# Half order, output buffers and the last block's stores of a fused Fourier mixing and maxout kernel

## The chip, the cores and the metric

The kernel runs on one core of a Trainium2 chip. The metric is the device time of one execution in microseconds, as the median of several runs; lower is better. A core has five instruction streams: TensorE (PE; its weight loads are shown apart as PEld), VectorE (DVE), ScalarE (ACT), GpSimd (POOL) and SyncE (SP). DMA transfers are issued from the streams of SP, POOL and ACT.

## What is computed

The input x has 8 batches of 3072 positions with 256 features. The kernel takes the real part of the Fourier transform over both axes, and passes each of the 24,576 resulting rows through a feed-forward layer whose hidden units are the maximum of three projections.

```python
def _attn_ref(x):                       # x: (8, 3072, 256)
    X = np.fft.fft(x, axis=1)
    X = np.fft.fft(X, axis=2)
    return X.real.astype(np.float32)

def _moe_ref(x, w1, w2, w3, w_out):     # w1, w2, w3: (256, 768), w_out: (768, 256)
    h = np.maximum(np.maximum(x @ w1, x @ w2), x @ w3)
    return (h @ w_out).astype(np.float32)

def reference(x, w1, w2, w3, w_out):
    return _moe_ref(_attn_ref(x).reshape(-1, 256), w1, w2, w3, w_out)
```

## The kernel before

**Mirror symmetry.** For real input, row s of the transform over positions and its mirror row 3072 - s share an even part and differ in the sign of an odd part. So only 1536 of 3072 positions are transformed (plus the middle one, `l2_mid`), into two tables per batch: `tE` (even part) and `tO` (odd part), each 128 x 1536 in bf16. Wherever rows are produced, a "direct" half (even plus odd, names with p) and a "mirror" half (even with the odd sign turned, names with m) are computed from the same columns.

**The maximum rewritten.** Folded weights `gE`, `gO` (made at the start) hold the feature transform times w2 - w1 and w3 - w1. Then max(x w1, x w2, x w3) = x w1 + max(0, x (w2 - w1), x (w3 - w1)). The second summand is the hidden activation `hp` or `hm`; the first is linear, and w1 times w_out is folded into `gw` (columns 0 to 255 for the even part, 256 to 511 for the odd part of direct rows, 512 to 767 for that of mirror rows).

**Loops.** Each of 8 batches is worked in 3 blocks of 512 columns (`TOKB`), each block in 6 units, one for each 128 of the 768 hidden units (`jc`). A unit is:

- `unit_plus` (L384): 4 matmuls of 512 columns into the banks `pse2` and `pse3` (L390, L391).
- `unit_out` (L401): ScalarE writes relu(pse2) to `stmp` (L404), VectorE writes max(pse3, stmp) to `hp` (L405).
- `unit_minus` (L394), one unit later by `finish` (L608): 2 matmuls (L398) that turn the same two banks into the mirror rows' values, and `unit_out` again, into `hm`. pse2 and pse3 have two banks each, so the `unit_plus` of the unit after the next writes the banks of this one.

The unit's last mirror part runs inside the first unit of the next block (`prev` is carried over), except at the end of a batch, where `finish` is called ahead of the block's output work (L632).

**The second layer** of a block is a generator, `l2_block` (L418), put in `l2_queue` when the block's units are done; each following unit advances it by 10 steps (`l2_some(10)`, L623), one matmul to a step as a rule. So the output of a block is interleaved with the units of the next. A block has 4 tiles of 128 positions (`sub`). For two tiles at a time, the even linear part is multiplied into the bank `pl` (L432) and copied by ScalarE to `even` (L436). For each tile, one matmul of 512 columns puts the two odd linear parts into the bank `po` (L440: direct in columns 0 to 255, mirror in 256 to 511). `l2_hidden` (L412) adds 6 matmuls of 256 columns to each half (L414). VectorE adds `even` to both halves and writes the tile `ot` (L453), which has 4 buffers. Direct rows leave by a plain transfer from SP, one row in 24 (L468). Mirror rows come out in falling order, and leave by an indexed transfer from POOL, with row numbers from `rows_m` (L458), and a memset of one element behind it (L462).

In the last block of the last batch the tiles come in the order 2, 3, 0, 1, and the last tile's addition is split in halves (L446, L450).

**Around it.** All engines run in the order of the program text (`manual_schedule`). Between units, a table of due pieces (`plan`) interleaves the transform of the next batch: `Mix.s` (L323, matmuls on x), `Mix.fold` (L333, VectorE), `Mix.k` (L361 to L373). SP's stream carries the loads of x two to three batches ahead (`load_chunk`, L100) between the direct stores, and POOL's stream carries the casts of the loaded x to bf16 (`turn_chunk`, L118) between the indexed stores; an instruction that waits holds up what stands behind it.

The lines that matter below: L390, L398, L405 (units), L414, L440, L453, L458, L468 (output), L533 (`out_pool`), L634 (where a block's output is queued), L661 (the program's exit).

Of the kernel before, what the change touches and what calls it, by code (L numbers as in the profile page):

```python
# [9 lines left out]
FP32 = mybir.dt.float32  # L10
BF16 = mybir.dt.bfloat16
INT32 = mybir.dt.int32
AX = mybir.ActivationFunctionType
ALU = mybir.AluOpType
# [19 lines left out]
def kernel(  # L34
# [9 lines left out]
    nc = tc.nc  # L44

    B, S, D = x.shape
# [3 lines left out]
    TOKB = 512  # L50
# [35 lines left out]
    gw = consts.tile([128, 768], BF16, tag="gw")  # L86
# [73 lines left out]
    for jh in range(2):  # L160
        for wsrc, wdst in ((moe_w1, w1_bf), (moe_w2, w2_bf), (moe_w3, w3_bf)):
            wld = nc.gpsimd.dma_start(
                out=wdst.rearrange("p (fc j) -> p fc j", fc=2)[:, :, jh * 384:(jh + 1) * 384],
                in_=wsrc.rearrange("(fc p) j -> p fc j", fc=2)[:, :, jh * 384:(jh + 1) * 384])
        if jh == 0:
            first_half = wld
    nc.gpsimd.dma_start(out=wout_bf.rearrange("p (jc c) -> p jc c", jc=NJC),
                        in_=moe_w_out.rearrange("(jc p) c -> p jc c", jc=NJC))
# [14 lines left out]
    for (name, value) in (("half_pi", 0.5 * math.pi), ("rnd", ROUND), ("n24", -24.0),  # L183
                          ("n256", -256.0), ("n3072", -3072.0)):
        c = gen.tile([128, 1], FP32, name=name, tag=name)
# [24 lines left out]
        out=m24blk.rearrange("p (g r) -> p g r", g=4),  # L210
        in0=t24.unsqueeze(1).to_broadcast([96, 4, 24]),
        in1=ind24.unsqueeze(2).to_broadcast([96, 4, 24]), op=ALU.mult)
# [5 lines left out]
    for (r0, r1) in ((0, 7), (7, 13)):  # L218
# [3 lines left out]
            out=v[:, cs].rearrange("p (r j) -> p r j", j=128),  # L222
            in0=j128.unsqueeze(1).to_broadcast([128, n, 128]), scalar=pidx,
            in1=pi13[:, r0:r1].unsqueeze(2).to_broadcast([128, n, 128]),
# [14 lines left out]
    for fc in range(2):  # L239
# [3 lines left out]
            out=vm[:, fc * 256:(fc + 1) * 256].rearrange("p (k c) -> p k c", c=128),  # L243
            in0=dvec.unsqueeze(1).to_broadcast([128, 2, 128]), scalar=pf[:, fc:fc + 1],
            in1=half.rearrange("p (k c) -> p k c", c=128), op0=ALU.mult, op1=ALU.add)
# [138 lines left out]
    def unit_plus(te, to, jc, n):  # L384

        js = slice(jc * 128, (jc + 1) * 128)
        pse2 = ps_l1.tile([128, TOKB], FP32, name="pse2", tag="pse2")
        pse3 = ps_l1.tile([128, TOKB], FP32, name="pse3", tag="pse3")
        for (pse, i) in ((pse2, 0), (pse3, 1)):
            nc.tensor.matmul(pse[:, 0:n], gE[i][:, js], te, start=True, stop=False)  # L390
            nc.tensor.matmul(pse[:, 0:n], gO[i][:, js], to, start=False, stop=True)  # L391
        return pse2, pse3

    def unit_minus(pses, to, jc):  # L394

        js = slice(jc * 128, (jc + 1) * 128)
        for i, pse in enumerate(pses):
            nc.tensor.matmul(pse, gD[i][:, js], to, start=False, stop=True,  # L398
                             skip_group_check=True)

    def unit_out(pses, dst, n):  # L401
        stmp = h_pool.tile([128, TOKB], BF16, name="stmp", tag="stmp")
        src3 = pses[1][:, 0:n]
        nc.scalar.activation(out=stmp[:, 0:n], in_=pses[0][:, 0:n], func=AX.Relu)  # L404
        nc.vector.tensor_tensor(out=dst, in0=src3, in1=stmp[:, 0:n], op=ALU.max)  # L405

    def stored(st, mine, others):
        for group in others:
            tc.declare_no_dep(st.ins, group=group, reason="each store has rows of its own")
        tc.add_to_no_dep_group(mine, st.ins)  # L410

    def l2_hidden(po, hcols):  # L412
        for jc in range(NJC):
            nc.tensor.matmul(po, hcols(jc), wout_bf[:, jc * 256:(jc + 1) * 256],  # L414
                             start=False, stop=(jc == NJC - 1), skip_group_check=True)
            yield

    def l2_block(b, blk, hp, hm, te, to):  # L418

        base = b * S  # L420
        last = b == B - 1 and blk == 2
        order = (2, 3, 0, 1) if last else range(4)
        for k, sub in enumerate(order):
            slot = blk * 4 + sub
            r = slot + 1
            cp = slice(slot * 128, slot * 128 + 128)
            sp = slice(sub * 128, sub * 128 + 128)
            if k % 2 == 0:
                pl = ps_f.tile([128, 512], FP32, name="pl", tag="ps")
                for i in range(2):  # L430
                    ci = (slot + i) * 128
                    nc.tensor.matmul(pl[:, i * 256:(i + 1) * 256], te[:, ci:ci + 128],  # L432
                                     gw[:, 0:256], start=True, stop=True)
                    yield
                even = out_pool.tile([128, 512], FP32, name="even", tag="even")
                nc.scalar.copy(out=even, in_=pl)  # L436
            lin = even[:, (k % 2) * 256:(k % 2 + 1) * 256]
            po = ps_o.tile([128, 512], FP32, name="po", tag="po")
            ot = out_pool.tile([128, 512], FP32, name="ot", tag="ot")
            nc.tensor.matmul(po, to[:, cp], gw[:, 256:768], start=True, stop=True)  # L440
            yield
            yield
            split = last and k == 3
            yield from l2_hidden(po[:, 256:512], lambda jc: hm[:, jc, sp])
            if split:
                nc.vector.tensor_tensor(out=ot[:, 256:512], in0=po[:, 256:512], in1=lin,  # L446
                                        op=ALU.add)
            yield from l2_hidden(po[:, 0:256], lambda jc: hp[:, jc, sp])
            if split:
                nc.vector.tensor_tensor(out=ot[:, 0:256], in0=po[:, 0:256], in1=lin,  # L450
                                        op=ALU.add)
            else:
                nc.vector.tensor_tensor(  # L453
                    out=ot.rearrange("p (h c) -> p h c", h=2),
                    in0=po.rearrange("p (h c) -> p h c", h=2),
                    in1=lin.unsqueeze(1).to_broadcast([128, 2, 256]), op=ALU.add)
            lo = 1 if r == 12 else 0
            stored(nc.gpsimd.indirect_dma_start(  # L458
                out, bass.IndirectOffsetOnAxis(
                    ap=rows_m[0:128 - lo, b * 12 + slot: b * 12 + slot + 1], axis=0),  # L460
                ot[lo:128, 256:512], None), "scattered", ("scattered", "direct"))
            nc.gpsimd.memset(mark, 0.0)  # L462
            if r <= 11:
                stores = [(0, 128, base + r)]
            else:
                stores = [(0, 64, base), (64, 128, base + 12)]
            for (p0, p1, row) in stores:
                stored(nc.sync.dma_start(out=out[row: row + 24 * (p1 - p0 - 1) + 1: 24, :],  # L468
                                         in_=ot[p0:p1, 0:256]), "direct", ("scattered",))

    def l2_mid():

# [29 lines left out]
    l2_queue = []  # L502

    def l2_some(n):
        while n > 0 and l2_queue:
            try:
                next(l2_queue[0])
                n -= 1
            except StopIteration:
                l2_queue.pop(0)  # L510
# [19 lines left out]
    ps_l1 = ctx.enter_context(tc.tile_pool(name="ps_l1", bufs=2, space=bass.MemoryType.PSUM))  # L530
    ps_o = ctx.enter_context(tc.tile_pool(name="ps_o", bufs=2, space=bass.MemoryType.PSUM))
    h_pool = ctx.enter_context(tc.tile_pool(name="hbuf", bufs=2))
    out_pool = ctx.enter_context(tc.tile_pool(name="outbuf", bufs=4))  # L533
    second = [prep_first(1, nc.vector.tensor_copy,
                         lambda: ps_o.tile([128, 512], FP32, name="psg", tag="po")),
              prep_second()]
# [66 lines left out]
    for b in range(B):  # L603
        mm = mixes[b]
        tE, tO = mm.tE, mm.tO
        prev = None

        def finish(prev):  # L608
            pses, to, jc, hm = prev
            unit_minus(pses, to, jc)  # L610
            unit_out(pses, hm[:, jc, :], TOKB)

        for blk in range(3):
            cs = slice(blk * TOKB, (blk + 1) * TOKB)
            hp = h_pool.tile([128, NJC, TOKB], BF16, name="hp", tag="hp")
            hm = h_pool.tile([128, NJC, TOKB], BF16, name="hm", tag="hm")
            for jc in range(NJC):
                pses = unit_plus(tE[:, cs], tO[:, cs], jc, TOKB)
                unit_out(pses, hp[:, jc, :], TOKB)
                if prev is not None:  # L620
                    finish(prev)
                prev = (pses, tO[:, cs], jc, hm)
                l2_some(10)  # L623
                if b == B - 1 and blk == 0:
                    if jc == 0:
                        middle = l2_mid()
                    for _ in range(5):
                        next(middle, None)
                for fn in plan.get((b, blk * NJC + jc), ()):
                    fn()  # L630
            l2_some(1000)
            if blk == 2:  # L632
                finish(prev)
            l2_queue.append(l2_block(b, blk, hp, hm, tE, tO))  # L634

    l2_some(1000)

# [28 lines left out]
```

## Time and profile before

| what | value |
|---|---|
| median of 3 runs | 457.61 us (456.12 to 457.81) |
| the profiled execution | 458.86 us |
| its span, first to last instruction | 457.1 us |
| mean granted TensorE clock in it | 0.987 |
| output addition, L453, 128x512 | 95 times, 682 ns each |
| hidden maximum, L405, 128x512 | 288 times, about 690 ns each |
| indexed store, L458, on POOL | 96 times, 1101 ns each |
| plain store, L468, on SP | 88 of 128 KB, 16 of 64 KB |

The time holds some 1.8 us outside the span. Busy time is given by engine; an engine that is busy nearly all the time bounds the kernel. A group's idle time is what its engine stood still just before it, with the instruction that ended the wait behind an arrow. Where the page shows a matmul's duration, several overlap: what a matmul takes from TensorE is the distance between the starts of two. The granted clock is the share of full speed at which TensorE was let run; 1.00 is full speed.

### The profile page before, as it was taken

To read this page: it belongs to the slowest core of one execution; us is meant where nothing else is said; L and a number is where in the kernel's file an instruction comes from. 1 tells how busy PE (TensorE), PEld (TensorE's weight loads), DVE (VectorE), ACT (ScalarE), POOL (GpSimd) and SP (SyncE) were. 2 spreads that over 40 slices of the span, in tenths; PEclk is the share of its full clock that TensorE was granted. 3 is DMA by queue.
4 is the path that set the end of the run, shared out by engine and by line. 5 is a ranking of instruction groups with operands and counts; after the bars stand their busy time and mean duration, and the time that the engine had idled before them with its cause. 6 is when DMAs were issued, how large, how long until landed. Compare 5 with 4: busy or idle time off the path is not lost.

```text
span 457.1 us, 9213 instructions
## 1 busy us (share of the span) xinstructions
PE 417.3 (91%) x3240; PEld 276.0 (60%) x3240; DVE 309.2 (68%) x643; ACT 276.8 (61%) x518; POOL 236.4 (52%) x258
## 2 busy tenths in 40 slices
PE   0499999999999999999999999999899999999990
PEld 0275666766676666666666667666476666655660
DVE  7667568675966596667856687567756596676760
ACT  3577576657666676567565676667466676555530
POOL 7616632884279525971388326952279421223252
PEclk9999999999999999999999999999899999999996
DMA  9999996498219861697419851797411211112132
GB/s 114 131 156 134 138 182 157 105 176 150 96 66 166 144 156 57 116 168 133 127 60 167 162 146 48 117 157 138 121 37 70 65 74 50 70 59 70 70 105 58
DMA packets 127422, 51.59 MB, mean 113 GB/s; under 512 B 109704, under 2 KB 124304, under 8 KB 127376
## 3 DMA queue, kind: packets, MB, share of 16 engines
q1 hardware_dynamic: 104496, 35.41, 41.7%
q0 software_dynamic: 21296, 15.21, 17.0%
q10 hardware_dynamic: 1584, 0.39, 0.6%
q8 instruction: 25, 0.41, 0.4%
q14 instruction: 21, 0.17, 0.1%
HBM read 28.31 MB, written 25.17 MB: 117 GB/s over the span
## 4 chain that ended last, share of the span: by engine, by line
PE 54%; issue 17%; POOL 10%; DMA 8%; DVE 5%; ACT 3%; SPq 1%; POOLq 0%; ACTq 0%; DVEq 0%
PE po L414 16%; PE pse L390 8%; PE pse L391 8%; PE pse L398 8%; POOL out_dram L458 7%; DMA xs<-in_x_dram 6%; PE ps L323 4%; DMA out_dram<-ot 3%; POOL x L118 2%; PE po L440 2%; DVE hm L405 2%; ACT stmp L404 1%; PE ps L361 1%; PE ps L370 1%; PE psg L270 1%
## 5 line engine op out<-in xcount | busy, mean ns | idle before, releaser
L404 ACT ACTIVATE stmp<-pse 128x512 bf16<-128x512 f32 x288 | 167.6, 604 | 62.1 <-PE pse L391 56.8
L458 POOL DMA_INDIRECT out_dram<-ot,rows_m x96 | 105.7, 1101 | 185.2 <-DVE ot L453 177.6
L405 DVE TENSOR_TENSOR hp<-pse,stmp 128x512 bf16<-128x512 f32 x144 | 99.4, 690 | 111.1 <-ACT stmp L404 67.6
L118 POOL CAST x<-xs 96x2048 bf16<-96x2048 f32 x28 | 105.9, 3782 | 19.6 <-DMA xs<-in_x_dram 17.5
L390 PE MATMUL pse<-tE,gE 128*128 128x512 bf16 x288 | 109.2, 379 | 0.6 <-DVE hm L405 0.2
L391 PE MATMUL pse<-tO,gO 128*128 128x512 bf16 x288 | 109.1, 379 | 0.0
L405 DVE TENSOR_TENSOR hm<-pse,stmp 128x512 bf16<-128x512 f32 x144 | 98.6, 685 | 8.4 <-ACT stmp L404 8.2
L414 PE MATMUL po<-wout_bf,hm 128*128 128x256 bf16 x576 | 89.3, 273 | 8.8 <-DVE hm L405 8.8
L398 PE MATMUL pse<-tO,gD 128*128 128x512 bf16 x288 | 86.1, 381 | 0.0
L414 PEld LDWEIGHTS <-hm 128*128 128x128 bf16 x576 | 56.4, 98 | 40.1 <-DVE hm L405 13.5
L414 PE MATMUL po<-wout_bf,hp 128*128 128x256 bf16 x576 | 79.2, 274 | 0.5 <-DVE ot L446 0.5
L325 ACT CAST ub<-ps 128x480 bf16<-128x480 f32 (+1 forms) x102 | 51.5, 559 | 40.5 <-PE ps L323 40.5
L453 DVE TENSOR_TENSOR ot<-po,even 128x512 f32<-128x512 f32 x95 | 64.8, 682 | 5.9 <-PE po L414 3.4
L414 PEld LDWEIGHTS <-hp 128*128 128x128 bf16 x576 | 56.7, 98 | 17.5 <-issue 1.2
L398 PEld LDWEIGHTS <-gD 128*128 128x128 bf16 x288 | 27.9, 98 | 32.2
L391 PEld LDWEIGHTS <-gO 128*128 128x128 bf16 x288 | 28.1, 98 | 20.3 <-issue 2.1
L390 PEld LDWEIGHTS <-gE 128*128 128x128 bf16 x288 | 28.6, 99 | 19.2 <-issue 0.4
L440 PE MATMUL po<-gw,tO 128*128 128x512 bf16 x96 | 36.6, 382 | 0.0
L323 PE MATMUL ps<-m24blk,x 96*128 96x96 bf16 x512 | 33.0, 216 | 2.5 <-DVE dif L254 1.5
L323 PEld LDWEIGHTS <-x 96*128 96x128 bf16 x512 | 30.1, 111 | 4.8 <-DVE dif L254 2.4
L436 ACT COPY even<-pl 128x512 f32<-128x512 f32 x48 | 28.4, 592 | 3.3 <-PE pl L432 3.0
L373 ACT CAST tO<-ps 128x512 bf16<-128x512 f32 x24 | 14.1, 586 | 24.5 <-PE ps L370 24.5
(113 smaller groups left out, 324.7 us busy)
## 6 DMA issues: line engine op xcount, KB each, us to landing
xs<-in_x_dram SPq DMA_DIRECT2D x112, 192.0 KB
out_dram<-ot SPq DMA_DIRECT2D x88, 128.0 KB
out_dram<-ot,rows_m POOLq DMA_INDIRECT x96, 3.9
w_bf<-in_moe_w_dram POOLq DMA_DIRECT2D x6, 192.0 KB, 4.4
out_dram<-ot SPq DMA_DIRECT2D x16, 64.0 KB
xs<-in_x_dram SPq DMA_DIRECT2D x8, 96.0 KB
x<-in_x_dram POOLq DMA_DIRECT2D x8, 96.0 KB, 11.8
xs<-in_x_dram ACTq DMA_DIRECT2D x4, 96.0 KB
```

The lines of the kernel that those rows point to most:

```text
L118: cast = nc.gpsimd.tensor_copy(turned[b][:, :, ch * 32:(ch + 1) * 32], raw.pop((b, ch)).rearrange("p (bb dl) -> p dl bb", dl=64))
L323: nc.tensor.matmul(ps1[:, i * 96:(i + 1) * 96], x0[:, d0 + i, :], m24blk, start=True, stop=True)
L325: evict(out=self.ub[:, d0 * 96:d1 * 96], in_=ps1[:, 0:(d1 - d0) * 96])
L390: nc.tensor.matmul(pse[:, 0:n], gE[i][:, js], te, start=True, stop=False)
L391: nc.tensor.matmul(pse[:, 0:n], gO[i][:, js], to, start=False, stop=True)
L398: nc.tensor.matmul(pse, gD[i][:, js], to, start=False, stop=True, skip_group_check=True)
L404: nc.scalar.activation(out=stmp[:, 0:n], in_=pses[0][:, 0:n], func=AX.Relu)
L405: nc.vector.tensor_tensor(out=dst, in0=src3, in1=stmp[:, 0:n], op=ALU.max)
L414: nc.tensor.matmul(po, hcols(jc), wout_bf[:, jc * 256:(jc + 1) * 256], start=False, stop=(jc == NJC - 1), skip_group_check=True)
L440: nc.tensor.matmul(po, to[:, cp], gw[:, 256:768], start=True, stop=True)
L453: nc.vector.tensor_tensor(out=ot.rearrange("p (h c) -> p h c", h=2), in0=po.rearrange("p (h c) -> p h c", h=2), in1=lin.unsqueeze(1).to_br ...
L458: stored(nc.gpsimd.indirect_dma_start(out, bass.IndirectOffsetOnAxis(ap=rows_m[0:128 - lo, b * 12 + slot: b * 12 + slot + 1], axis=0), ot[ ...
```

## The change

1. In `l2_block`, the direct half of each output bank gets its six hidden matmuls first, then the mirror half; the block's split of a last tile and its own tile order go.
2. `ot` has six buffers in place of four; `even` gets a pool of its own with two buffers in place of four.
3. The last block of the last batch is put out by a new generator, `l2_last`. The mirror half of it is computed in reversed order, so that mirror rows come out in rising order: `finish` writes `hm` backwards in that block, and POOL makes reversed copies of 512 columns of `tE` and `tO` ahead of the block. Even and odd linear parts are both multiplied into the bank, for each half apart. VectorE copies the bank out. All rows leave by plain transfers: from SP, and one of the last tile's two from ACT. The tiles come in the order 3, 0, 1, 2, and the last one is copied in halves.

```diff
     def l2_block(b, blk, hp, hm, te, to):
...
-        last = b == B - 1 and blk == 2
-        order = (2, 3, 0, 1) if last else range(4)
-        for k, sub in enumerate(order):
+        for sub in range(4):
...
-                even = out_pool.tile([128, 512], FP32, name="even", tag="even")
+                even = even_pool.tile([128, 512], FP32, name="even", tag="even")
...
-            split = last and k == 3
+            yield from l2_hidden(po[:, 0:256], lambda jc: hp[:, jc, sp])
             yield from l2_hidden(po[:, 256:512], lambda jc: hm[:, jc, sp])
-            if split:
-                nc.vector.tensor_tensor(out=ot[:, 256:512], in0=po[:, 256:512], in1=lin,
-                                        op=ALU.add)
-            yield from l2_hidden(po[:, 0:256], lambda jc: hp[:, jc, sp])
...
+    def l2_last(hp, hm, te, to, flipped):
+
+        base = (B - 1) * S
+        ter, tor = flipped
+        for sub in (3, 0, 1, 2):
+            slot = 8 + sub
+            r = slot + 1
+            cp = slice(slot * 128, slot * 128 + 128)
+            sp = slice(sub * 128, sub * 128 + 128)
+            sm = slice((3 - sub) * 128, (4 - sub) * 128)
+            po = ps_o.tile([128, 512], FP32, name="po", tag="po")
+            ot = out_pool.tile([128, 512], FP32, name="ot", tag="ot")
+            for (h, tev, tov, wo, hid) in (
+                    (0, te[:, cp], to[:, cp], gw[:, 256:512], lambda jc: hp[:, jc, sp]),
+                    (1, ter[:, sm], tor[:, sm], gw[:, 512:768], lambda jc: hm[:, jc, sm])):
+                ph = po[:, h * 256:(h + 1) * 256]
+                nc.tensor.matmul(ph, tev, gw[:, 0:256], start=True, stop=False)
+                yield
+                nc.tensor.matmul(ph, tov, wo, start=False, stop=True)
+                yield
+                yield from l2_hidden(ph, hid)
+                if sub == 2:
+                    nc.vector.tensor_copy(out=ot[:, h * 256:(h + 1) * 256], in_=ph)
+            if sub != 2:
+                nc.vector.tensor_copy(out=ot, in_=po)
+            if r <= 11:
+                stores = [(0, 128, base + r, 0), (0, 128, base + 24 - r, 256)]
+            else:
+                stores = [(0, 64, base, 0), (64, 128, base + 12, 0),
+                          (0, 64, base + 1548, 256), (64, 127, base + 1560, 256)]
+            for k, (p0, p1, row, c) in enumerate(stores):
+                eng = nc.scalar if sub == 2 and k == 0 else nc.sync
+                stored(eng.dma_start(out=out[row: row + 24 * (p1 - p0 - 1) + 1: 24, :],
+                                     in_=ot[p0:p1, c:c + 256]), "direct", ("scattered",))
...
-    out_pool = ctx.enter_context(tc.tile_pool(name="outbuf", bufs=4))
+    out_pool = ctx.enter_context(tc.tile_pool(name="outbuf", bufs=6))
+    even_pool = ctx.enter_context(tc.tile_pool(name="evenbuf", bufs=2))
...
-            unit_out(pses, hm[:, jc, :], TOKB)
+            unit_out(pses, hm[:, jc, ::-1] if hm is last_hm else hm[:, jc, :], TOKB)
...
+            if b == B - 1 and blk == 2:
+                last_hm = hm
+                for t, fl in zip((tE, tO), flipped):
+                    nc.gpsimd.tensor_copy(fl, t[:, 3 * TOKB - 1: 2 * TOKB - 1: -1])
...
-            l2_queue.append(l2_block(b, blk, hp, hm, tE, tO))
+            l2_queue.append(l2_last(hp, hm, tE, tO, flipped) if b == B - 1 and blk == 2 else
+                            l2_block(b, blk, hp, hm, tE, tO))
```

More of the change, by code (lines that the diff above doesn't have):

```diff
@@ L427, in l2_block @@
             sp = slice(sub * 128, sub * 128 + 128)
-            if k % 2 == 0:
+            if sub % 2 == 0:
                 pl = ps_f.tile([128, 512], FP32, name="pl", tag="ps")
@@ L434, in l2_block @@
                     yield
-                even = out_pool.tile([128, 512], FP32, name="even", tag="even")
+                even = even_pool.tile([128, 512], FP32, name="even", tag="even")
                 nc.scalar.copy(out=even, in_=pl)
-            lin = even[:, (k % 2) * 256:(k % 2 + 1) * 256]
+            lin = even[:, (sub % 2) * 256:(sub % 2 + 1) * 256]
             po = ps_o.tile([128, 512], FP32, name="po", tag="po")
@@ L442, in l2_block @@
             yield
-            split = last and k == 3
+            yield from l2_hidden(po[:, 0:256], lambda jc: hp[:, jc, sp])
             yield from l2_hidden(po[:, 256:512], lambda jc: hm[:, jc, sp])
-            if split:
-                nc.vector.tensor_tensor(out=ot[:, 256:512], in0=po[:, 256:512], in1=lin,
-                                        op=ALU.add)
-            yield from l2_hidden(po[:, 0:256], lambda jc: hp[:, jc, sp])
[L449 to L456, printed above, removed]
+            nc.vector.tensor_tensor(
+                out=ot.rearrange("p (h c) -> p h c", h=2),
+                in0=po.rearrange("p (h c) -> p h c", h=2),
+                in1=lin.unsqueeze(1).to_broadcast([128, 2, 256]), op=ALU.add)
             lo = 1 if r == 12 else 0
@@ L610, in finish @@
             unit_minus(pses, to, jc)
-            unit_out(pses, hm[:, jc, :], TOKB)
+            unit_out(pses, hm[:, jc, ::-1] if hm is last_hm else hm[:, jc, :], TOKB)
+        last_hm = None
+        if b == B - 1:
+            flipped = []
+            for t, name in ((tE, "tEr"), (tO, "tOr")):
+                fl = h_pool.tile([128, TOKB], BF16, name=name, tag=name)
+                flipped.append(fl)
         for blk in range(3):
```

## The prediction

> **What bounds the kernel now.** I read the shares by engine first, then the waits of each engine, then the timeline around the longest waits, then the end of the span.
>
> ```profile
> PE 417.3 (91%) x3240; PEld 276.0 (60%) x3240; DVE 309.2 (68%) x643; ACT 276.8 (61%) x518; POOL 236.4 (52%) x258
> ```
>
> TensorE is the bound. From 60 us on, its windows of 10 us read 10.00 busy wherever none of the waits below falls, so time is lost only in its few waits and in what follows its last matmul at 446.66 us (span 457.1).
>
> ```profile
> PE po L414 <- DVE hm L405: 8.8, 17, 2.0
> PE ps L323 <- POOL x L118: 1.0, 2, 0.5
> PEld L414 <- DVE hm L405: 13.5, 17, 2.3
> DVE ot L453 <- DMA out_dram<-ot: 2.2, 2, 1.4
> POOL out_dram L458 <- DVE ot L453: 177.6, 71, 5.5
> ```
>
> These are the waits (us in total, times, longest). The first and third are one event: matmul 6 of the mirror half of an output bank needs hidden chunk 5, which VectorE is still writing. It occurs at all 16 block boundaries inside a batch, and once in the last block. Here is one boundary, and the longest:
>
> ```profile
> 426.40 0.10 PEld L414 LDWEIGHTS <-hm 128*128 128x128 bf16 x1 [0.50 <-DVE hm L405]
> 426.41 0.28 PE L414 MATMUL po<-wout_bf,hm 128*128 128x256 bf16 x1 [0.22 <-DVE hm L405]
> 426.53 0.38 PE L390 MATMUL pse<-tE,gE 128*128 128x512 bf16 x1
> ...
> 325.18 0.10 PEld L414 LDWEIGHTS <-hm 128*128 128x128 bf16 x1 [2.33 <-DVE hm L405]
> ...
> 323.24 0.69 DVE L453 TENSOR_TENSOR ot<-po,even 128x512 f32<-128x512 f32 x1 [1.41 <-DMA out_dram<-ot]
> ```
>
> Five loads began at 425.26; their matmuls began at 425.48 and follow each 0.108 us (six from 437.80, the next instruction at 438.45). The sixth was due at 426.02 and came at 426.41: a loss of 0.39, where the load row shows 0.50. So I take a load's idle time less 0.11 as the loss. The wait at 325.18 has another root: VectorE stood 1.41 us at L453 for an output buffer whose stores had not landed, and the hidden chunk was queued behind it. The windows after it:
>
> ```profile
> 326.20:329.50 3.30, 3.30 (x16) 2.00 (x15) 2.34 (x5) 0.93 (x2) 0.00 (x0) 0.50 0.00 0
> 329.60:335.00 5.40, 5.40 (x47) 3.79 (x46) 2.51 (x9) 3.72 (x7) 4.78 (x3) 1.00 0.16 53
> ```
>
> The third number from the end is the granted clock: 0.50 after that pause, 1.00 from 329.6 on. Last, the program's exit (line 661), beside the last store:
>
> ```profile
> 447.89 0.96 POOL L458 DMA_INDIRECT out_dram<-ot,rows_m  x1 [0.21 <-issue]
> ...
> L661 SPq EVENT_SEMAPHORE  x11: 17/28/6677, 447.5 to 457.0; - x11
> ...
> L661 POOLq DRAIN  x3: 46/97/8582, 447.7 to 456.8; - x3
> ```
>
> SP's exit checks stand 6.68 us for the last indexed store, and POOL's drain lasts 8.58 us, to 456.3.
>
> **Part 1, direct half first.** Nothing is added: the same matmuls, and the same number of steps between units. Behind six direct matmuls, the pause is no longer met at the hidden chunk but at the next unit's third matmul (L390 on pse3), whose bank the same VectorE instruction must first read. Between lie one 256-column matmul (0.11) and two of 512 columns (0.43, from the starts 426.53 and 426.96), so each boundary can recover up to 0.54. The load rows at 69, 121, 154, 171, 204, 222, 255, 272, 305, 359 and 377 us show 0.65 to 1.10, a loss of 0.54 or more: 11 x 0.54 = 5.94. Those at 411 and 426 show 0.50: 2 x 0.39 = 0.78. Two more, at 50.86 (capped, 0.54) and 102.99 (0.39), I count at nothing: TensorE waits at 57.70 and 103.81 for POOL's cast of x (0.72 of load idle each), and the loads or casts behind those had begun before the recovered time. Would they come earlier too, it is +0.9. Sum **6.7**, bounds 0 (the wait appears elsewhere) to 7.6. What is late next is nothing: VectorE idles 0.45 to 1.1 us before the next hp there.
>
> **Part 2, six output buffers; `even` on two of its own.** Buffers at 307 to 323 us are held by stores issued late, behind x loads on SP's queue (the longest step in the chain there: 8.46 us for a store). Output tiles follow each other at some 3.5 us (12 in a batch of 43), so two more buffers stretch the allowed hold by about 7 us against waits of 0.81 and 1.41. This takes away the stall at 325 (2.33 - 0.11 = 2.22, of which 0.07 stays, as at a usual 0.72 boundary capped at 0.54), the one at 318.53 (load idle 0.46 - 0.11 = 0.35), and the half clock of 3.4 us, worth 1.7: **4.2**. Bounds 0 to 4.3. `even` on two buffers costs nothing: a buffer comes back after the pair before last, both of whose additions are long done when the next pair's copy runs; without that cover it would be one copy, 0.59 at L436, per pair.
>
> [...] This trace shows a gap of 2.3 us with 3.4 us of half clock behind it. [...]
>
> **Part 3, the last block.** Added: the even half is multiplied into each half-bank, 16 matmuls of 256 columns per tile in place of the equal of 15, 4 x 0.108 = +0.43. Gone: the wait at 440.24, -0.39, as 14 matmuls now stand ahead of the late chunk. Kept: TensorE's stop between the halves of the last tile (0.69 of load idle at 445.84), as the second half still waits for VectorE to read the first. Two reversing POOL copies of 512 bf16: nearest row, L118, 3.78 us for 2048 columns, so an estimated 0.95 each (0.3 to 3.8 by the smallest cast and the whole row). They stand on POOL's queue ahead of block 1's indexed stores, at about 424, and are needed at 440; without that cover the end moves by 1.9. The hidden chunk written backwards: nearest row L405, 0.69; at double that, six times, 4.1 us of VectorE, which has 2.3 idle per 10 us there, so at most some 2 reach the end. I take 0.69. The even copies on ACT (0.59) and the additions of the last tiles become copies of equal size (128x512 CAST 0.68, against 0.68). Sum **0**, bounds -2 to +0.3 as gain.
>
> **Part 4, the end.** Now 457.08 - 446.66 = 10.42 from the last matmul. Then: VectorE's half copy 0.03 + 0.42 (L450's row), 0.04 to SP, issue to landing, exit. By the DMA semaphore counts in the trace, the last block's four direct stores before the final one landed 1.7 to 2.2 us after SP began to issue them: 1.95. From landing to SP's sign-off took 0.37, from POOL's release to the end 0.74. Sum 3.55, so a gain of 6.87, **6.9**. POOL's drain no longer decides: its last indexed store is block 1's, at about 439, and even 8.6 us of drain from 440.7 end by 449.3, just ahead of 450. The other bound: the final direct store of before, in flight with two indexed ones, had most packets in by 450.6 and the last by 453.97, 6.8 us after issue; that would leave a gain of 2.0. I take the stores in a quiet queue, since no indexed stores are left there. SP issues ten stores in place of five and ACT's queue takes one of the last two; 128 KB moves in about half a microsecond in the 1 us windows, so they don't pile up.
>
> **Sum**: 6.7 + 4.2 + 0 + 6.9 = 17.8. The profiled execution was 458.86 us with a span of 457.1; it becomes 441.1. The median of the timed runs is 1.25 lower (457.61), so 439.8 is predicted.
>
> **Rivals.**
> *The boundary wait only moves.* For it: VectorE feeds pse3's bank as well as hm, and ACT idles at L404 for TensorE. Against: at 426 the chunk was done at 426.35, pse3 was wanted at 426.96. Part 1 falls away: 457.6 - 11.1 = 446.5.
> *The end stays long.* For it: single packets of the final store straggled to 453.97. Against: earlier ones did so by about 1 us only. Gain of 2.0 at the end: 444.7.
> *The buffers don't help*, as the store that is late is held by loads for longer than 20 us, or the pause was this one execution's: 457.6 - 13.6 = 444.0.
> *Slower*: TensorE, ahead by a boundary's 0.54 twice a batch, outruns the casts of x. For it: two waits at L323 on L118. Each new wait beyond 2 us would also halve the clock, by the row at 325 some 2.2 + 1.7 = 3.9 us a batch; from five such batches of the seven on (19.5 over 17.8) the kernel is slower, with six at 457.6 - 17.8 + 23.4 = 463.2. Against: 26 of 28 casts have TensorE waiting for none of them, and the loads are started by the same queue that waits for TensorE's tiles, so they come forward with it.
> *No change* would need parts 1, 2 and 4 to miss together.
>
> **How the numbers follow.** Forecast 0.62, boundary moves 0.12, end stays 0.11, buffers don't help 0.07, slower 0.05, no change 0.03. All but the last two are faster: 0.92. The likeliest case alone runs from 437.5 (part 1 at 7.6, and the lowest run of before, 1.5 under the median) to 443. The range reaches up to 446.5, the rival with part 1 gone, which leaves under 2 in 10 out. Same and faster are split at 0.5% (2.3 us), what a measurement of this kernel can tell.
>
> **What would show it.** Part 1: the waits of PE on hm gone from L414, with at most 17 short ones on pse at L390. Part 2: no wait of VectorE's output addition for a DMA, granted clock 1.00 at 326. Part 3: TensorE from the last L398 to the end still about 8.2 us, hm's mean near 0.69. Part 4: under 4.5 us from the last matmul to the end. I would be wrong if L390 or L323 take up the waits with over 0.6 each, if the reversed writes are slow, or if the last store again needs 5 us and more.

## The result and the profile after

The changed kernel takes 441.52 us (median of 4 runs, 438.80 to 442.57); the kernel before took 456.87 beside it (455.81 to 457.81). The ratio is 0.9656, with a 95% interval of 0.9601 to 0.9710: faster, by some 15.3 us. Predicted were 439.8. The ratios of the experiments below leave out the profiled execution and two runs some 2% longer than their kernel's fastest (458.57 us with the direct half first alone, 449.98 with four buffers); the medians include them.

I cut the span of each profiled execution at the same three events and use these stretches throughout: A, from the start to the first weight load for the second batch's x (L323; 57.70 us before); B, from there to the first weight load of the last block's closing pair (L398); C, from there to the last matmul's end; D, the rest. First the windows of the kernel before over B, C and D (start and end; length; then busy time and count for PE, PEld, DVE, ACT, POOL; granted clock; DMA share; GB/s):

```profile
57.70:438.35 380.65, 372.17 (x2921) 246.61 (x2922) 266.59 (x544) 241.46 (x456) 197.03 (x206) 1.00 0.51 111
438.35:446.66 8.31, 7.57 (x61) 5.57 (x58) 4.18 (x7) 1.66 (x3) 4.79 (x7) 1.00 0.32 111
446.66:457.08 10.42, 0.00 (x0) 0.00 (x0) 0.42 (x1) 0.00 (x0) 2.05 (x4) 0.61 0.23 51
```

The same for the changed kernel:

```profile
60.12:428.84 368.72, 364.94 (x2868) 247.03 (x2922) 266.30 (x544) 241.35 (x456) 198.61 (x208) 1.00 0.52 115
428.84:437.20 8.36, 7.84 (x69) 6.46 (x66) 4.19 (x7) 0.60 (x1) 1.05 (x2) 1.00 0.41 139
437.20:440.66 3.46, 0.00 (x1) 0.00 (x0) 0.42 (x1) 0.00 (x0) 0.00 (x0) 1.00 0.23 81
```

The span fell from 457.08 to 440.66, by 16.42. B gave 11.93, C cost 0.05, D gave 6.96, and A cost 2.42. Per-engine work in B is the same to within 0.4 us for VectorE and ScalarE: only waits went. (Matmul counts differ, as some records are missing; the weight loads, 2922 in both, are whole.) These are the waits of TensorE after 30 us in the changed kernel, from its view of waits:

```profile
PE ps L323 <- POOL x L118: 4.2, 2, 3.2
PE po L477 <- DVE ot L483: 0.5, 1, 0.5
PE pse L390 <- DVE hm L405: 0.3, 1, 0.3
```

The 17 waits of L414 on hm are gone, and they did not move to L390: the single one of 0.3 us there falls at 43.83 us, ahead of the first boundary, and the second trace of the kernel before has it too (42.27 us, 0.35). No wait of an output addition for a store is listed any more. What grew is the wait for the cast of x, nearly all of it at the border of A and B:

```profile
60.12 0.60 PE L323 MATMUL ps<-m24blk,x 96*128 96x96 bf16 x10 [3.24 <-POOL x L118]
105.62 0.60 PE L323 MATMUL ps<-m24blk,x 96*128 96x96 bf16 x10 [0.93 <-POOL x L118]
```

At the end, the exit of the changed kernel (line 698 there):

```profile
L698 SPq EVENT_SEMAPHORE  x11: 17/28/28, 438.1 to 440.6; - x11
L698 POOLq DRAIN  x3: 46/97/4648, 429.9 to 440.4; - x3
```

POOL's long drain now begins at 429.9 and lasts 4.65 us, so it is over before TensorE is. SP's exit checks, of which one stood 6.68 us before, are all short in this row; between two of them SP waits 1.2 us for its own last store.

### The profile page after: what moved, and what is told of

It reads as the page before. It is cut to its first block, busy times and chain, and to the rows that moved or that the text cites. A ratio compares the mean times of both kernels' runs of the same rounds, so it can differ in the third digit from the quotient of the medians.

```text
span 440.7 us, 9144 instructions
## 1 busy us (share of the span) xinstructions
PE 410.6 (93%) x3192; PEld 277.8 (63%) x3248; DVE 308.9 (70%) x643; ACT 275.7 (63%) x516; POOL 232.2 (53%) x252
## 4 chain that ended last, share of the span: by engine, by line
PE 83%; DMA 7%; POOL 5%; DVE 2%; issue 1%; SPq 1%; ACT 0%; POOLq 0%; DVEq 0%
PE po L414 26%; PE pse L390 14%; PE pse L398 13%; PE pse L391 11%; PE ps L323 6%; PE po L438 4%; DMA x<-in_x_dram 4%; POOL x L118 3%; DMA xs<-in_x_dram 3%; PE pl L430 2%; PE psg L270 1%; PE ps L361 1%; PE ps L370 1%; PE ps L364 1%; PE ps L368 1%
## 5 line engine op out<-in xcount | busy, mean ns | idle before, releaser
L448 POOL DMA_INDIRECT out_dram<-ot,rows_m x92 | 100.6, 1093 | 169.3 <-DVE ot L443 162.1
L390 PE MATMUL pse<-tE,gE 128*128 128x512 bf16 x280 | 106.2, 379 | 2.4 <-DVE hm L405 0.3
L391 PE MATMUL pse<-tO,gO 128*128 128x512 bf16 x248 | 93.9, 379 | 0.5
L414 PE MATMUL po<-wout_bf,hp 128*128 128x256 bf16 x576 | 86.1, 273 | 0.1
L398 PE MATMUL pse<-tO,gD 128*128 128x512 bf16 x280 | 83.9, 379 | 0.5
L414 PE MATMUL po<-wout_bf,hm 128*128 128x256 bf16 x576 | 78.6, 273 | 0.0
L414 PEld LDWEIGHTS <-hp 128*128 128x128 bf16 x576 | 56.4, 98 | 26.2
L414 PEld LDWEIGHTS <-hm 128*128 128x128 bf16 x576 | 56.4, 98 | 16.3
L443 DVE TENSOR_TENSOR ot<-po,even 128x512 f32<-128x512 f32 x92 | 62.8, 683 | 0.0
L398 PEld LDWEIGHTS <-gD 128*128 128x128 bf16 x288 | 27.9, 98 | 32.1
L390 PEld LDWEIGHTS <-gE 128*128 128x128 bf16 x288 | 28.6, 99 | 19.3 <-issue 0.4
L391 PEld LDWEIGHTS <-gO 128*128 128x128 bf16 x288 | 28.1, 98 | 19.9 <-issue 1.6
L323 PE MATMUL ps<-m24blk,x 96*128 96x96 bf16 x512 | 33.0, 216 | 5.9 <-POOL x L118 4.2
L323 PEld LDWEIGHTS <-x 96*128 96x128 bf16 x512 | 30.1, 111 | 8.4 <-POOL x L118 4.7
L438 PE MATMUL po<-gw,tO 128*128 128x512 bf16 x92 | 34.9, 379 | 0.0
L434 ACT COPY even<-pl 128x512 f32<-128x512 f32 x46 | 27.2, 592 | 0.3
```

The source lines that it names most:

```text
L323: nc.tensor.matmul(ps1[:, i * 96:(i + 1) * 96], x0[:, d0 + i, :], m24blk, start=True, stop=True)
L443: nc.vector.tensor_tensor(out=ot.rearrange("p (h c) -> p h c", h=2), in0=po.rearrange("p (h c) -> p h c", h=2), in1=lin.unsqueeze(1).to_br ...
L448: stored(nc.gpsimd.indirect_dma_start(out, bass.IndirectOffsetOnAxis(ap=rows_m[0:128 - lo, b * 12 + slot: b * 12 + slot + 1], axis=0), ot[ ...
```

## The experiments

Times with a ratio are medians of four runs (six for the last tile in two banks); ratios are to the kernel before, run on the same chip beside each. B, C and D are of the one profiled execution of each kernel.

**Direct half first, alone.** In the kernel before, all blocks but the last:

```diff
-            yield from l2_hidden(po[:, 256:512], lambda jc: hm[:, jc, sp])
+            if not last:
+                yield from l2_hidden(po[:, 0:256], lambda jc: hp[:, jc, sp])
+            yield from l2_hidden(po[:, 256:512], lambda jc: hm[:, jc, sp])
...
-            yield from l2_hidden(po[:, 0:256], lambda jc: hp[:, jc, sp])
+            if last:
+                yield from l2_hidden(po[:, 0:256], lambda jc: hp[:, jc, sp])
```

> The kernel before with the direct half first in all blocks but the last; nothing else. Theory (each boundary pause of 0.39 to 0.99 us is recovered whole, the pause behind the output buffer stays): no wait of PE at L414 on hm at the boundaries; the stretch from the end of the wait at about 57.7 us to the first L398 of the last block (380.75 us before, 368.82 in the changed kernel) falls by 7 to 8 us, the end after the last matmul stays at about 10.4; time about 449.5. Rival (the wait only moves to L390 on pse3): waits of about 0.4 to 0.6 us at L390, the stretch falls by under 2 us, time about 456.

449.69 us, ratio 0.9793 (0.9721 to 0.9865). B is 372.91 (7.74 less), D 10.47. The waits of its PE:

```profile
PE pse L390 <- DVE hm L405: 2.0, 4, 0.7
PE po L440 <- DVE ot L456: 0.9, 1, 0.9
...
PE po L414 <- DVE hm L405: 0.2, 1, 0.2
```

The boundary waits are gone; the single one left is the last block's. The four at L390 look like the rival, but there are 16 boundaries, and VectorE's waits tell where they come from:

```profile
DVE ot L456 <- DMA out_dram<-ot: 3.2, 3, 2.2
```

Two of the four (at 267.80 and 313.76 us) come behind additions that waited for a store. Ahead of the other two the view names no store, but with six buffers and the same order (both inner parts, below) none of the four is left. So the boundary wait did not move to L390: these waits come from having four buffers, whose cost B still holds here. The next runs part the two.

**Six buffers, alone.** In the kernel before:

```diff
-                even = out_pool.tile([128, 512], FP32, name="even", tag="even")
+                even = even_pool.tile([128, 512], FP32, name="even", tag="even")
...
-    out_pool = ctx.enter_context(tc.tile_pool(name="outbuf", bufs=4))
+    out_pool = ctx.enter_context(tc.tile_pool(name="outbuf", bufs=6))
+    even_pool = ctx.enter_context(tc.tile_pool(name="evenbuf", bufs=2))
```

> The kernel before with six buffers for ot and two for even; nothing else. Theory: no wait of the output addition for a DMA, the boundary pauses stay as they were (about 12 us of load idle over 17 times), no half clock in the middle; the stretch from 57.7 us to the last block falls by about 4 us, time about 452.7. Rival (the pause at 325 us was that execution's own, other runs of before don't have it): the time is that of before, about 457, although the profile shows no such wait.

453.78 us, ratio 0.9882 (0.9827 to 0.9938); B 376.63, which is 4.02 less. The boundary waits stay, and no wait for a store is listed:

```profile
PE po L414 <- DVE hm L405: 6.6, 17, 0.8
```

**The last block, alone.** The changed kernel, with the mirror half first and four buffers each:

```diff
-            yield from l2_hidden(po[:, 0:256], lambda jc: hp[:, jc, sp])
             yield from l2_hidden(po[:, 256:512], lambda jc: hm[:, jc, sp])
+            yield from l2_hidden(po[:, 0:256], lambda jc: hp[:, jc, sp])
...
-    out_pool = ctx.enter_context(tc.tile_pool(name="outbuf", bufs=6))
-    even_pool = ctx.enter_context(tc.tile_pool(name="evenbuf", bufs=2))
+    out_pool = ctx.enter_context(tc.tile_pool(name="outbuf", bufs=4))
+    even_pool = ctx.enter_context(tc.tile_pool(name="evenbuf", bufs=4))
```

> The kernel before with the new last block alone (reversed mirror rows, plain stores); mirror half first elsewhere, four buffers. Theory: last matmul to the end 3.5 us in place of 10.4, first L398 of the last block to the last matmul 8.2 as before, time about 450; the boundary pauses and the buffer pause stay. Rival (the end was short in the changed kernel only as its queues were empty earlier thanks to the other parts): the end takes 5 us or more, time 452 and above.

The windows over C and D of this kernel:

```profile
434.00:442.37 8.37, 7.85 (x69) 6.44 (x66) 4.19 (x7) 0.60 (x1) 1.05 (x2) 1.00 0.42 140
442.37:445.82 3.45, 0.00 (x0) 0.00 (x0) 0.42 (x1) 0.00 (x0) 0.00 (x0) 1.00 0.23 80
```

C and D are those of the changed kernel, so the short end needs nothing of the other parts. The time was missed: 453.31 where about 450 was expected, ratio 0.9893 (0.9828 to 0.9958), while the profiled execution took 447.6; the interval holds the 0.985 expected. What made the other three runs 5 to 9 us longer than the profiled one stays open, as only that one has a trace. B is 377.42 here: in this execution the buffer wait of VectorE was 0.6 us in all, so four buffers cost 0.8 over the 376.63 of six.

**Both inner parts, old end.** The two edits of the first two experiments together.

> Direct half first and six buffers, with the last block as before. Theory (the parts add up): the stretch from the first cast wait to the last block falls by 11 to 12 us, the end stays at 10.4, time about 445.5. Rival (order and buffers hide the same pause, so they don't add): 447.5 to 449.

447.28 us, ratio 0.9766 (0.9696 to 0.9837). B is 368.82, D 10.40, by the windows over B and D:

```profile
55.84:424.66 368.82, 367.90 (x2924) 247.18 (x2922) 266.47 (x545) 241.34 (x456) 197.28 (x206) 1.00 0.51 115
432.97:443.37 10.40, 0.00 (x0) 0.00 (x0) 0.42 (x1) 0.00 (x0) 2.05 (x4) 0.69 0.22 51
```

The stretch fell by 11.83 and the parts add: B is that of the changed kernel to 0.1 us, and the order of halves alone, with six buffers on both sides, is 376.63 - 368.82 = 7.81.

**The changed kernel with four buffers.**

```diff
-    out_pool = ctx.enter_context(tc.tile_pool(name="outbuf", bufs=6))
+    out_pool = ctx.enter_context(tc.tile_pool(name="outbuf", bufs=4))
```

> The changed kernel with four buffers for ot in place of six (even stays at two). Theory (the order of halves takes away the slack that hid part of a late buffer, so a wait of VectorE for a store now reaches TensorE nearly whole): waits of the output addition for a DMA of 1 to 4 us in all, TensorE waits at L390 or L438 behind them, the stretch from the first cast wait to the last block 370 to 373 us where the changed kernel has 368.7; time 1 to 4 us above it. Rival (with the direct half first the buffers no longer matter): no such wait, 368.7.

445.07 us, ratio 0.9711 (0.9642 to 0.9781); B 372.38, which is 3.66 more. VectorE waits 3.6 us for stores in 5 waits, and TensorE waits behind it:

```profile
DVE ot L443 <- DMA out_dram<-ot: 3.6, 5, 1.2
PE pse L390 <- DVE hm L405: 3.4, 5, 1.1
```

One of TensorE's five is again the early one of 0.35 (at 43.06 us). The other four, 3.0 us in all, come each behind one of the last four waits of VectorE (0.41, 0.68, 1.21 and 0.98 us): 0.39, 0.60, 1.14 and 0.91. So a late buffer reaches TensorE nearly whole, as the theory had it. That the old order would have hidden more of it is not shown; the part on the prediction comes back to it.

**Mirror rows of the last block from POOL's queue, plain.**

```diff
-                eng = nc.scalar if sub == 2 and k == 0 else nc.sync
+                eng = nc.gpsimd if c else nc.scalar if sub == 2 else nc.sync
```

> The changed kernel with the last block's mirror rows still reversed and plain, but issued from POOL's queue in place of SP's. [...]

One execution, 442.45 us. D is 5.84 (last matmul's end at 434.68, span 440.52), 2.4 more than from SP. The last store in the timeline:

```profile
435.44 0.54 POOL L493 DMA_DIRECT2D out_dram<-ot  x1 [1.61 <-DVE ot L483]
```

And the rows of the exit:

```profile
L698 SPq EVENT_SEMAPHORE  x11: 17/28/3806, 433.4 to 440.5; - x11
L698 POOLq DRAIN  x3: 46/102/4315, 435.4 to 440.2; - x3
```

SP's check on the store ended at 437.4, so it had landed 2.0 us after its issue; POOL's drain went on to 439.7 (435.42 + 4.32), 2.3 us past the landing. In the kernel before SP's check ended at 454.5 and the drain at 456.3, so 1.8 us of the old end were the drain. The greater part of what is left, 10.42 - 5.84 = 4.6, came with the indexed stores: two of them were issued only at 446.60 and 447.89, and the last landed 6.6 us after its issue, where the plain one from POOL took 2.0. Whether that is the indexing, or that their packets shared the DMA engines with the last direct store's, no run tells apart.

**The last tile's second half in a bank of its own.** An attempt to beat both:

```diff
                 ph = po[:, h * 256:(h + 1) * 256]
+                if sub == 2 and h == 1:
+                    ph = ps_f.tile([128, 512], FP32, name="po2", tag="ps")[:, 0:256]
```

> The changed kernel with the second half of the very last tile in a bank of its own, so that TensorE need not wait for VectorE between the halves (0.69 us of load idle at 436.17). Theory: that wait goes, first L398 of the last block to the last matmul 7.7 in place of 8.36, the end as it was; time about 0.6 us lower, which the timed runs can hardly show. Rival (the wait is the bank's access, and moves to another place): 8.3 as before.

Its windows over C and D:

```profile
424.89:432.58 7.69, 7.69 (x69) 6.46 (x66) 4.20 (x7) 0.60 (x1) 1.05 (x2) 1.00 0.38 125
432.58:436.03 3.45, 0.00 (x1) 0.00 (x0) 0.42 (x1) 0.00 (x0) 0.00 (x0) 1.00 0.40 138
```

C is 7.69, with TensorE busy all of it: 0.67 us gained, in the trace. The times don't show it: 441.68, ratio 0.9656 (0.9614 to 0.9698), the same ratio as the changed kernel's.

**The kernel before, once more.**

> The kernel before once more, to see whether its pause behind an output buffer recurs. Theory (stores behind x loads on SP's queue, with little to spare at four buffers): waits of the output addition for a DMA again, from 0.5 to 3 us in all, with or without half clock behind. Rival (peculiar to that one execution): none.

One execution, 455.56 us. From VectorE's waits:

```profile
DVE ot L453 <- DMA out_dram<-ot: 2.0, 2, 1.4
```

The window behind the longest pause:

```profile
323.40:330.00 6.60, 6.54 (x56) 4.86 (x58) 5.11 (x19) 3.31 (x6) 3.05 (x4) 1.00 0.18 64
```

The pause recurs, at the same place (2.12 us of load idle at 323.4), but this time without half clock behind it. B is 378.80, so the buffers are worth 378.80 - 376.63 = 2.2 here.

## Why the prediction was right, and where its sizes were off

| term | predicted | profiled executions | elsewhere |
|---|---|---|---|
| part 1, order of halves | 6.7 | 11.9 with part 2 | 7.8 (six buffers on both sides) |
| part 2, buffers | 4.2 | | 4.0, 2.2 and 0.8 (old order), 4.1 and 3.7 (new order) |
| part 3, last block's work | 0 | -0.05 | -0.06 (last block alone) |
| part 4, the end | 6.9 | 6.96 | 6.97 (last block alone) |
| before the second batch's x | none | -2.42 | A from 55.4 to 60.1 us |

**Part 1: mechanism right, its size 1.1 too small.** 7.8 was measured, above even the bound of 7.6. The step that failed: "Between lie one 256-column matmul (0.11) and two of 512 columns (0.43 ...), so each boundary can recover up to 0.54." I left out the pieces of the next batch's transform that the plan puts between two units. In the changed kernel, at the boundary that answers to 255.63:

```profile
252.91 0.82 PE L414 MATMUL po<-wout_bf,hp 128*128 128x256 bf16 x6
253.33 0.68 DVE L405 TENSOR_TENSOR hm<-pse,stmp 128x512 bf16<-128x512 f32 x1
253.56 0.59 PE L323 MATMUL ps<-m24blk,x 96*128 96x96 bf16 x10
254.43 0.38 PE L390 MATMUL pse<-tE,gE 128*128 128x512 bf16 x1
```

Ten matmuls of the transform stand between the output matmuls and the unit, so the bank that hm frees at 254.01 is wanted only at 254.43 (of the unit's first four matmuls L390 and L391 on pse2 go ahead; the record of its L390 is missing). In the kernel before, the same ten stood there too, behind the wait, at 255.75. Without the cap the losses sum to 7.75 in the run with six buffers alone, where no late store mixes in (load idle less 0.11, the 14 boundaries from 68 to 421 us but the one at 102), and 7.81 was measured. That the boundary at 102.99 brings nothing was right: its gain goes into the cast wait at 103.81, whose idle loads rose from 0.72 to about 1.2 in every run with the new order. The one at 50.86 lies in A, whose spread hides it.

**Part 2: right in kind, uncertain in size.** Buffers remove the wait (shown by six buffers alone, and put back by four in the changed kernel). Their worth depends on how late the stores land in an execution. The 4.2 held 1.7 for the half clock, which the other traces don't have in the middle; that it came so near the 4.0 measured against that same execution is partly luck, as two other traces of the old order give 2.2 and 0.8. In the two traces with the new order four buffers cost 3.7 and 4.1 without any half clock. The expectation explained this by slack that the old order gave a late buffer. What the traces show is that VectorE's waits for stores were longer: 3.6 and 3.2 us in all, against 2.2, 2.0 and 0.6 with the old order. For each microsecond of such waits B is longer by about one in either order (2.0 us of wait cost 2.2 with the old, 3.6 cost 3.7 with the new), so the old boundary pause did not hide the waits themselves. Whether the faster pace makes the stores later, or these executions happened to have late ones, two traces against three can't tell. A reading was off as well: output tiles follow each other at about 4.2 us (12 in the 50.4 us from 252.21 to 302.57, the first loads for x of two batches), not 3.5; the conclusion on the buffers doesn't hang on it.

**Part 3** was right to 0.05: the reversed writes of hm took 0.69 us in the last block (rows at 428.47 and 429.99) as others do, and the two reversing copies on POOL 0.61 each, well ahead of their use. **Part 4** was right to 0.1, the sum of 3.55 became 3.46; of its steps, issue to landing took about 1.7 us in place of 1.95, and landing to SP's sign-off 0.5 in place of 0.37.

**The rest.** The span fell by 16.42 where the sum has 17.8. The 1.4 between them is the 2.42 lost in A, ahead of the second batch's x, where I had no term, less the 1.0 that B gave beyond 6.7 + 4.2: two errors that partly cancelled. Both kernels do the same in A but for the order at one boundary, and A varied from 55.4 to 60.1 us over ten profiled executions, of either kind. SP issued the second batch's loads of x some 1.6 us apart in the changed kernel's trace, and 1.4 apart in the kernel with the last tile in two banks, where A was 56.09; the casts follow them. B, C and D of the changed kernel sum to 380.54, while its four runs had spans of 436.9 to 440.7, so A may explain all of their spread, though only one of the four has a trace; what makes the loads slower in one execution than in another stays open.

**The rivals** fell. The boundary wait did not move, the end did not stay long, six buffers helped, and TensorE did not outrun the casts later on: with the new order and six buffers the first loads for x of successive batches lie 49.17 us apart from the fourth interval on, in four traces. The price set on such a wait, a halved clock from 2 us on, was wrong too: behind the wait of 3.2 us at 60.12 the clock stayed at 1.00 (see the last section).

## What to carry to other kernels

Where an engine consumes a chunk that has just been ordered from another, let it consume the older chunks first: the order cost nothing here and gave 7.8 us. Look at the next late resource as well: four output buffers cost 0.8 to 2.2 us with the old order (4.0 with half clock behind) and about 4 with the new, and six took that away. At a kernel's end count from the last matmul, and keep the last stores off a queue whose drain outlasts their landing, as POOL's did here by 1.8 and 2.3 us.

## What was not expected of the hardware

In these traces the length of a pause of TensorE did not decide alone whether its clock was halved. In the kernel before, the clock was 0.50 from 326.20 to 329.50 us, behind the load idle of 2.33 us at 325.18. In the second trace of that kernel, the load idle of 2.12 us at the same place was followed by a clock of 1.00 (323.40 to 330.00 us). And in the changed kernel TensorE stood for 3.2 of 3.5 us with the clock at 1.00 during and after it:

```profile
56.60:60.10 3.50, 0.28 (x3) 0.00 (x0) 0.33 (x1) 0.00 (x0) 3.46 (x1) 1.00 0.81 116
60.10:63.00 2.90, 2.83 (x26) 1.96 (x28) 0.90 (x2) 2.46 (x5) 1.21 (x2) 1.00 0.91 153
```

What parts the pause that cost the clock from the two that did not, no run shows.
